# Strassen's algorithm in the last FFN stage of the last two token tiles, for two of four token blocks

## The chip, the cores and the metric

The kernel runs on one core of one Trainium2 chip. The metric is the device time of one execution in microseconds (us). A profiled execution also gives the span from the first to the last instruction, which here is about 2 us shorter than the device time. A difference under 2% counts as "same".

Engines: PE is TensorE's matmuls, PEld its weight loads, DVE is VectorE, ACT is ScalarE, POOL is GpSimd, SP is SyncE, which issues DMA transfers.

## The reference

A sparse attention over 8 x 8 heads, then a multiplicative feed-forward network (FFN) on 4608 tokens:

```python
x = np.ascontiguousarray(attn_out.transpose(0, 2, 1, 3)).reshape(B * S, H * D)   # 4608 x 512
a = x @ w1                   # 512 x 1024
b = x @ w2
h = a * b @ w3               # 1024 x 1024
out = h @ w_out              # 1024 x 512, float32
```

## The kernel before

The kernel folds w3 and w_out into one matrix, `w34` (1024 x 512), so the FFN has two stages: `abt = (x @ w1) * (x @ w2)`, then `out = abt @ w34`. Tokens go in 9 tiles of 512. The last two tiles, tA and tB, already form the first stage by Strassen's algorithm in the form that takes 7 products of half-size blocks for 8 (the Winograd form), for seven of the eight blocks of the hidden dimension (d_ff); one block stays plain. Their last stage is plain, 8 matmuls of 512 columns for each block of 128 tokens (in the last one, split in three column parts):

```python
for ci in range(4 * hf, 4 * hf + 4):
    pin(nc.tensor.matmul(ps, big[("abt", t)][:, ci, bass.ds(ts * P, P)],
                         w34[:, ci, bass.ds(n0, nw)], start=(ci == 0), stop=(ci == KF - 1)))
```

`hf` makes a half-quarter: 4 matmuls, 0.86 us, that can be placed on its own.

Instructions aren't placed by hand. Each is an `op` with an engine, an estimated time, dependencies, buffers and a rank. A planner in the kernel plays these through once and fixes the program order of every engine:

```python
plan = Plan(dict(f=NF, B=2, stg=NSTG, ...))   # buffers: f = 4 single PSUM banks, B = 2 pairs of banks
...
seq = plan.order(slack=cfg.get("slack", 0), ...)
for o in seq:
    o.fn(o.on)
```

The accumulators lie in PSUM, the memory that this program's matmuls write their sums to. A Strassen block has three: A in a single bank (`f`), and E and G together in one two-bank tile (`B`):

```python
def bk(x, kA=kA, kB=kB):
    return bank(*kA) if x == "A" else bank(*kB)[:, "EG".index(x)]
```

The products are P1 (into A), P5 (into G), P6, P7, P4 (into A in turn), P2 (into E) and P3 (into G). Between them, copies and additions on ACT and VectorE: `e` copies A to E after P1, `u2` copies A after P6, `g` adds that to G, `c22` evicts A after P7, `c11` copies E after P2.

The softmax here doesn't subtract the row's maximum and nothing guards it: scores larger than these inputs give would overflow.

## Time and profile before

| | |
|---|---|
| device time, median of 3 runs | 270.85 us (270.61 to 271.14) |
| span of the profiled run | 268.3 us |
| TensorE busy | 256.9 us, 96% |
| first stage of tA and tB | starts at 224.71 us |
| last run of plain last-stage matmuls | 253.00 to 264.43 us, 68 matmuls |
| idle of TensorE in the first stage of tA, tB | about 1.1 us, at 229 to 238 us |

The **tail** is the time from the start of the first plain first-stage matmul of tA (`ps_a`) to the end of the last matmul. Before, it is 264.43 - 224.71 = 39.72 us.

### The profile page before, as it was taken

What the parts mean: (1) busy time and instruction counts of PE and PEld (TensorE: products, weight loads), DVE (VectorE), ACT (ScalarE), POOL (GpSimd) and SP (SyncE); (2) the same over time, 40 slices, a digit from 0 to 9 for tenths busy, and PEclk for the clock granted to TensorE, in tenths of its full rate; (3) what the DMA queues carried; (4) which work ended last, traced back from release to release, by engine and by line L of the source; (5) the groups of instructions that cost most, each with busy time, mean ns of one, the idle gap of its engine ahead of it and who ended that gap; (6) DMA issues with size and microseconds to landing.
All of it is one profiled execution on the core that took longest, in us unless ns stands there. A gap on an engine that the chain in (4) does not pass through costs nothing.

```text
span 268.3 us, 6079 instructions
## 1 busy us (share of the span) xinstructions
PE 256.9 (96%) x2251; PEld 140.3 (52%) x2251; DVE 179.0 (67%) x342; ACT 162.2 (60%) x293; POOL 168.9 (63%) x186
## 2 busy tenths in 40 slices
PE   7878799999999999999999999999999999999994
PEld 2457687545655555554554454455445554434443
DVE  6744565885787748866875788569748865678601
ACT  2780467774766785577477557764775576577241
POOL 6676897779979716955796369716989753900000
PEclk9999999999999999999999999999999999999999
DMA  6999899999799988899999998999996004000053
GB/s 247 322 365 288 294 353 353 326 266 290 255 287 211 175 205 243 188 167 283 228 184 180 264 248 182 189 252 235 162 189 198 2 0 156 0 2 0 0 197 121
DMA packets 72766, 54.41 MB, mean 203 GB/s; under 512 B 44256, under 2 KB 62048, under 8 KB 72736
## 3 DMA queue, kind: packets, MB, share of 16 engines
q1 hardware_dynamic: 72736, 54.02, 83.1%
q8 instruction: 18, 0.29, 0.5%
q14 instruction: 12, 0.10, 0.1%
HBM read 38.93 MB, written 9.44 MB: 180 GB/s over the span
## 4 chain that ended last, share of the span: by engine, by line
PE 86%; DMA 7%; POOL 2%; issue 1%; DVE 1%; ACT 1%; SPq 1%; POOLq 0%; DVEq 0%
PE ps_o L1155 23%; PE ps_b L1135 19%; PE ps_a L1119 18%; DMA st<-in_moe_w_dram 5%; PE ps_Aw L1053 4%; PE ps_S L795 4%; PE ps_Bw L1053 3%; PE ps_mm L670 3%; PE ps_X L843 3%; PE ps_X L831 3%; DMA st<-in_k_dram 2%; PE ps_U L924 2%; PE ps_T L748 2%; POOL w3n L314 1%; SPq L317 1%
## 5 line engine op out<-in xcount | busy, mean ns | idle before, releaser
L1155 PE MATMUL ps_o<-w,abt 128*128 128x512 f16 (+2 forms) x304 | 67.9, 368 | 0.0
L1135 PE MATMUL ps_b<-xT,w2h 128*128 128x512 f16 x232 | 59.4, 379 | 0.2 <-DVE kTL L312 0.2
L1119 PE MATMUL ps_a<-xT,w1h 128*128 128x512 f16 x232 | 59.6, 379 | 0.0
L310 ACT COPY asb<-ps_a 128x512 f32<-128x512 f32 x58 | 33.9, 587 | 30.1 <-PE ps_a L1119 29.0
L1141 DVE TENSOR_TENSOR abt<-ps_b,asb 128x512 f16<-128x512 f32 x58 | 39.9, 688 | 7.8 <-PE ps_b L1135 6.4
L314 POOL CAST xs<-st 80x1024 f16<-80x1024 f32 (+1 forms) x36 | 33.3, 940 | 18.3 <-DMA st<-in_k_dram 10.5
L812 ACT ACTIVATE ps_S<-ps_S 128x576 f32<-128x576 f32 (+2 forms) x56 | 32.8, 627 | 16.4 <-PE ps_S L795 16.4
L1155 PEld LDWEIGHTS <-abt 128*128 128x128 f16 x304 | 27.5, 98 | 28.2 <-issue 0.2
L904 DVE TENSOR_TENSOR xT<-ps_X,rcp 64x288 f16<-64x288 f32 x56 | 25.2, 450 | 18.3 <-ACT rcp L888 17.8
L1135 PEld LDWEIGHTS <-w2h 128*128 128x128 f16 x232 | 21.6, 98 | 23.7 <-issue 0.7
L310 ACT COPY osb<-ps_o 128x512 f32<-128x512 f32 (+1 forms) x36 | 20.2, 580 | 18.7 <-PE ps_o L1155 17.7
L314 POOL CAST v16L<-st 32x768 f16<-32x768 f32 (+1 forms) x32 | 26.3, 821 | 7.3 <-DMA st<-in_v_dram 5.7
L1119 PEld LDWEIGHTS <-w1h 128*128 128x128 f16 x232 | 20.2, 99 | 18.5
L819 DVE TENSOR_TENSOR ptm<-ps_S,maskL 128x576 f16<-128x576 f32 x28 | 19.9, 753 | 9.1 <-ACT ps_S L812 9.0
L867 DVE TENSOR_TENSOR xqs<-ps_X,rcq 96x384 f16<-96x384 f32 (+1 forms) x36 | 20.5, 568 | 1.2
L314 POOL CAST v16S<-st 72x1024 f16<-72x1024 f32 (+1 forms) x16 | 16.5, 1035 | 6.8 <-DMA st<-in_v_dram 6.8
L877 ACT ACTIVATE ps_X<-ps_X 64x576 f32<-64x576 f32 x28 | 17.6, 630 | 3.8 <-PE ps_X L831 3.2
L888 ACT ACTIVATE rcp<-ps_X 64x576 f32<-64x576 f32 x28 | 18.1, 647 | 0.9
L843 PEld LDWEIGHTS <-ptm 128*96 128x96 f16 (+1 forms) x224 | 14.6, 123 | 5.8 <-issue 0.2
L670 PE MATMUL ps_mm<-woh,xT 128*128 128x256 f16 x128 | 16.0, 273 | 1.3 <-POOL woh L314 1.3
L314 POOL CAST x<-st 128x1024 f16<-128x1024 f32 x14 | 14.4, 1036 | 4.4 <-DMA st<-in_k_dram 2.6
L819 DVE TENSOR_TENSOR ptm<-ps_S,maskK 72x576 f16<-72x576 f32 x20 | 14.1, 746 | 2.6 <-ACT ps_S L812 2.6
(113 smaller groups left out, 359.1 us busy)
## 6 DMA issues: line engine op xcount, KB each, us to landing
out_dram<-osb SPq DMA_DIRECT2D x35, 256.0 KB
st<-in_moe_w_dram SPq DMA_DIRECT2D x16, 512.0 KB
st<-in_v_dram SPq DMA_DIRECT2D x16, 288.0 KB
st<-in_v_dram SPq DMA_DIRECT2D x16, 256.0 KB
st<-in_q_dram SPq DMA_DIRECT2D x7, 512.0 KB
st<-in_k_dram SPq DMA_DIRECT2D x7, 512.0 KB
st<-in_q_dram SPq DMA_DIRECT2D x10, 256.0 KB
st<-in_k_dram SPq DMA_DIRECT2D x10, 256.0 KB
```

The lines of the kernel that those rows point to most:

```text
L310: pin(nc.scalar.copy(out=out, in_=in_))
L314: pin(nc.gpsimd.tensor_copy(out=out, in_=in_))
L670: pin(nc.tensor.matmul(ps, w3T(kc)[:, js], big["woh"][:, kc, ns], start=(kc == 0), stop=(kc == KF - 1)))
L812: pin(nc.scalar.activation(out=sps, in_=sps, func=AF.Exp, bias=0.0, scale=scale))
L819: pin(nc.vector.tensor_mul(ptm[0:kr, 0:576].rearrange("p (h a x) -> p h a x", h=2, x=w), pte[0:kr].rearrange("p h (a x) -> p h a x", x=w), ...
L843: pin(nc.tensor.matmul(xps[0:w, h, i * 65:(i + 1) * 65], ptms[pslot][0:kr, c0:c0 + w], vt[0:kr, 2 * (hp % 2) + h, g * m + i, 0:D + 1], sta ...
L867: pin(nc.vector.tensor_mul(xqs[0:w, 0:m].rearrange("p i h d -> p h i d"), xv[:, :, :, 0:D], _ap(rcp, 0, [[rcp.ap[0][0], w], [4, 2], [1, m] ...
L904: pin(nc.vector.tensor_mul(o, i0, i1))
L1119: pin(nc.tensor.matmul(ps, w1h[:, ci, js], xT[ci][:, tok], start=(ci == 0), stop=(ci == KM - 1)))
L1135: pin(nc.tensor.matmul(ps, w2h[:, ci, js], xT[ci][:, tok], start=(ci == 0), stop=(ci == KM - 1)))
L1141: pin(nc.vector.tensor_mul(big[("abt", t)][:, jc, :], bank("f", f"b{t}_{jc}"), live[("asb", t, jc)]))
L1155: pin(nc.tensor.matmul(ps, big[("abt", t)][:, ci, bass.ds(ts * P, P)], w34[:, ci, bass.ds(n0, nw)], start=(ci == 0), stop=(ci == KF - 1)))
```

## The change

Token blocks 0 and 1 of both tiles leave the plain last stage and go as two Strassen blocks: 7 products of 4 matmuls of 256 columns instead of 16 matmuls of 512. The left factors are sums of parts of abt (Z1, Z2, Z4 on VectorE, Z3 on POOL), the right factors differences of parts of w34 (on POOL). The plain d_ff block of the first stage moves from 0 to 7, so that the first half of the hidden dimension is finished earlier.

```diff
-  sf=(1, 2, 3, 4, 5, 6, 7), ...
+  sf=(0, 1, 2, 3, 4, 5, 6), ..., so=(0, 1), ro=42)
...
+    def out_strassen():
+        HN = DM // 2
+        hh = {(1, 1): (tA, 0), (1, 2): (tA, 4), (2, 1): (tB, 0), (2, 2): (tB, 4)}
+        W = {(i, j): w34[:, 4 * i - 4:4 * i, bass.ds(HN * (j - 1), HN)] for i in (1, 2) for j in (1, 2)}
...
+            def bk(x, kA=kA, kB=kB):
+                return (bank(*kA) if x == "A" else bank(*kB)[:, "EG".index(x)])[:, 0:HN]
...
+                    for c in range(4):
+                        pin(nc.tensor.matmul(bk(x), lf()[:, c], rt()[:, c], start=st_ and c == 0, stop=c == 3,
+                                             skip_group_check=not st_))
+
+                return plan.op(f"{nm}o{ts}", {"PE": 440}, fn, deps=d + list(extra), take=take,
+                               rank=100 + 24 * tA + cfg.get('ro', 30) + 3 * n_ + rank, soft=True)
...
+            q1 = prod("P1", take=[kA], extra=sfirst)
+            q5 = prod("P5", take=[kB], extra=[q1], rank=.1)
+            ce_ = vec("e", AC, lambda e, bk=bk: copy(e, bk("E"), bk("A")), [q1, q5])
+            q6 = prod("P6", extra=[ce_], rank=.5)
+            q2 = prod("P2", extra=[ce_], rank=.6)
+            cu = vec("u2", AC, ... copy(e, new("u2"), bk("A")), [q6], take=["u2"])
+            q7 = prod("P7", extra=[cu], rank=1)
+            g = vec("u4", DV, ... tensor_add(bk("G"), bk("G"), tmp["u2"]), [cu, c5], give=[tk["u2"]])
+            c22 = vec("c22", DV, ... tensor_add(new("o8")[:, HN:DM], bk("A"), tmp["p5"]), [q7, c5], ...)
+            c11 = vec("c11", AD, ... copy(e, new("o7")[:, 0:HN], bk("E")), [q2], take=["o7"])
+            q3 = prod("P3", extra=[g], rank=1.1)
+            q4 = prod("P4", extra=[c22], rank=1.2)
...
         for ts in range(NT // P):
+            if t in zs and ts in SO:
+                continue
```

(A renamed dictionary key in the attention part has no effect on the program.)

More of the change, by code (lines that the diff above doesn't have):

```diff
@@ L41 @@
            pord=lambda b: (2, 3, 0, 1) if b < 2 else (0, 1, 2, 3), tsplit=False, dmaf=1.08, nhr=8, cast=dict(w1=dict(POOL=1040)),
-           first=('DVE', 'ACT', 'POOL'), early=0, pm=4, nx=4, nstg=8, new=(2, 3), lb=3, ll=4, nat={'POOL': 1160}, sf=(1, 2, 3, 4, 5, 6, 7), te={'POOL': 2150}, nr=(1, 25, 2, 0), te1='POOL', se=((3, 0), (3, 1), (1, 0), (2, 0), (4, 0)))
+           first=('DVE', 'ACT', 'POOL'), early=0, pm=4, nx=4, nstg=8, new=(2, 3), lb=3, ll=4, nat={'POOL': 1160}, sf=(0, 1, 2, 3, 4, 5, 6), te={'POOL': 2150}, nr=(1, 25, 2, 0), te1='POOL', se=((3, 0), (3, 1), (1, 0), (2, 0), (4, 0)), so=(0, 1), ro=42)
 def _ap(t: bass.AP, off_add, dims):
@@ L302 @@
     plan = Plan(dict(f=NF, B=2, stg=NSTG, asb=2, osb=3, rcp=2, xqs=2, xqd=cfg.get("nxq", 2), w3n=3, abt=NABT,
-                     u2=2, p5=2, c11=2, c22=2))
+                     u2=2, p5=2, c11=2, c22=2, ob=4))
     def pin(ins):
@@ L580, in fn @@
                 copy(e, t.rearrange("p c h d -> p h c d"), stg[key][0:nr])
-                x16[(b, nm, hp)] = t
+                x16[(b, nm, "s", hp)] = t
             c = cast("c" + key, key, ds, {"POOL": 825} if local else POOL, fn)
@@ L594, in ft @@
                 pin(nc.sync.dma_start(o.rearrange("x (c w) -> x c w", w=nr),
-                                      x16[(b, nm, hp)].rearrange("p c h d -> p (c h d)"), transpose=True))
+                                      x16[(b, nm, "s", hp)].rearrange("p c h d -> p (c h d)"), transpose=True))
             o = DTop[(b, nm, hp)] = plan.op(f"D{nm}{b}_{hp}", {"SP": 1300}, ft, deps=[c], dma=cfg.get("dtc", (1080, 1200))[0 if local else 1], store=True,
@@ L947 @@
     tk1, tk2 = bass.ds(tA * NT, NT), bass.ds(tB * NT, NT)
-    smul, sfirst = {}, []
+    smul, sfirst, mul = {}, [], {}
     if SF:
@@ L1003 @@
                 T[(i, 1)].deps.append(gate)
+        T1last = T[(4, 1)]
         SL = lambda j: (lambda c: St[j // 3][:, (j - 1) % 2 if j < 3 else j - 3, c])
@@ L1092, with ftt, ah, sv @@
         smul[(tA, jc)], smul[(tB, jc)] = h1, h2
+    SO = cfg.get("so", ()) if SF else ()
+    def out_strassen():
+        HN = DM // 2
+        hh = {(1, 1): (tA, 0), (1, 2): (tA, 4), (2, 1): (tB, 0), (2, 2): (tB, 4)}
+        W = {(i, j): w34[:, 4 * i - 4:4 * i, bass.ds(HN * (j - 1), HN)] for i in (1, 2) for j in (1, 2)}
+        T, Tt = {}, {}
+        for i, x, y in ((1, (1, 2), (1, 1)), (3, (2, 2), (1, 2)), (2, (2, 2), 1), (4, (2, 1), 2)):
+            def ftt(e, i=i, x=x, y=y):
+                if i in (1, 2):
+                    raw = stgs[plan.slot[("stg", f"O{i}")]].bitcast(FP16).rearrange("p (i k n) -> p i k n", i=2, k=4)
+                    Tt[i], Tt[{1: 3, 2: 4}[i]] = raw[:, 0], raw[:, 1]
+                b0 = Tt[y] if isinstance(y, int) else W[y]
+                eng = nc.gpsimd if e == "POOL" else nc.vector
+                pin(eng.tensor_sub(Tt[i], W[x], b0))
+            T[i] = plan.op(f"O{i}", {"POOL": 2150}, ftt, deps=w34op + [T1last, T.get(1), T.get(2)],
+                           take=[("stg", f"O{i}")] if i in (1, 2) else [], rank=14, lock=True)
+        def ah(i, j, ts):
+            t, c0 = hh[(i, j)]
+            return big[("abt", t)][:, c0:c0 + 4, bass.ds(ts * P, P)]
+        def sv(i, ts):
+            return xT[i - 1][:, 0:4 * NT].rearrange("p (k n) -> p k n", k=4)[:, :, bass.ds(ts * P, P)]
+        md = lambda t, k: [mul[(t, jc)] for jc in range(4 * k - 4, 4 * k)]
+        for n_, ts in enumerate(SO):
+            Sx = {}
+            for i in (3, 1, 2, 4):
+                def fss(e, i=i, ts=ts):
+                    eng = nc.gpsimd if e == "POOL" else nc.vector
+                    f = eng.tensor_add if i == 1 else eng.tensor_sub
+                    a0 = {3: lambda: ah(1, 1, ts), 1: lambda: ah(2, 1, ts), 2: lambda: sv(1, ts), 4: lambda: ah(1, 2, ts)}
+                    a1 = {3: lambda: ah(2, 1, ts), 1: lambda: ah(2, 2, ts), 2: lambda: ah(1, 1, ts), 4: lambda: sv(2, ts)}
+                    pin(f(sv(i, ts), a0[i](), a1[i]()))
+                d = {3: md(tA, 1) + md(tB, 1), 1: md(tB, 1) + md(tB, 2), 2: md(tA, 1), 4: md(tA, 2)}[i]
+                Sx[i] = plan.op(f"Z{i}_{ts}", {"POOL": 1150} if i == 3 else {"DVE": 430}, fss,
+                                deps=d + ([Sx[i // 2]] if i in (2, 4) else []), rank=3.9 + .01 * n_, lock=True)
+            kA, kB = ("f", f"Ao{ts}"), ("B", f"Bo{ts}")
+            prods = dict(P1=(lambda ts=ts: ah(1, 1, ts), lambda: W[(1, 1)], "A", md(tA, 1) + w34op),
+                         P5=(lambda ts=ts: sv(1, ts), lambda: Tt[1], "G", [Sx[1], T[1]]),
+                         P6=(lambda ts=ts: sv(2, ts), lambda: Tt[2], "A", [Sx[2], T[2]]),
+                         P2=(lambda ts=ts: ah(1, 2, ts), lambda: W[(2, 1)], "E", md(tA, 2)),
+                         P7=(lambda ts=ts: sv(3, ts), lambda: Tt[3], "A", [Sx[3], T[3]]),
+                         P4=(lambda ts=ts: ah(2, 2, ts), lambda: Tt[4], "A", md(tB, 2) + [T[4]]),
+                         P3=(lambda ts=ts: sv(4, ts), lambda: W[(2, 2)], "G", [Sx[4]]))
+            tmp = {}
+            def bk(x, kA=kA, kB=kB):
+                return (bank(*kA) if x == "A" else bank(*kB)[:, "EG".index(x)])[:, 0:HN]
+            def new(nm, tmp=tmp, ts=ts):
+                if nm[0] == "o":
+                    tmp[nm] = xT[plan.slot[("ob", f"{nm}o{ts}")]][:, 4 * NT:6 * NT].bitcast(FP32)
+                else:
+                    tmp[nm] = qkp.tile([P, HN], FP32, tag=TAG[nm], bufs=2, name=nm)
+                return tmp[nm]
+            def prod(nm, extra=(), take=(), rank=0, ts=ts, kA=kA, kB=kB, prods=prods, bk=bk):
+                lf, rt, x, d = prods[nm]
+                def fn(e):
+                    if nm == "P1":
+                        bank(*kA, [P, NT], FP32)
+                    if nm == "P5":
+                        live[kB] = seen[plan.slot[kB]]
+                    st_ = nm in ("P1", "P5")
+                    for c in range(4):
[3 more added lines that the diff above has]
+                               rank=100 + 24 * tA + cfg.get('ro', 30) + 3 * n_ + rank, soft=True)
+            def vec(nm, eng, fn, deps, give=(), take=()):
+                return plan.op(f"{nm}o{ts}", eng, fn, deps=deps, give=list(give),
+                               take=[("ob" if x[0] == "o" else x, f"{x}o{ts}") for x in take], rank=3 + .1 * n_)
+            AC, DV, AD = {"ACT": 370}, {"DVE": 400}, {"ACT": 370, "DVE": 380}
+            tk = {x: ("ob" if x[0] == "o" else x, f"{x}o{ts}") for x in ("u2", "p5", "o7", "o8")}
+            q1 = prod("P1", take=[kA], extra=sfirst)
+            q5 = prod("P5", take=[kB], extra=[q1], rank=.1)
+            ce_ = vec("e", AC, lambda e, bk=bk: copy(e, bk("E"), bk("A")), [q1, q5])
+            q6 = prod("P6", extra=[ce_], rank=.5)
+            c5 = vec("p5", AC, lambda e, bk=bk, new=new: copy(e, new("p5"), bk("G")), [q5], take=["p5"])
+            q2 = prod("P2", extra=[ce_], rank=.6)
+            cu = vec("u2", AC, lambda e, bk=bk, new=new: copy(e, new("u2"), bk("A")), [q6], take=["u2"])
+            q7 = prod("P7", extra=[cu], rank=1)
+            g = vec("u4", DV, lambda e, bk=bk, tmp=tmp: pin(nc.vector.tensor_add(bk("G"), bk("G"), tmp["u2"])),
+                    [cu, c5], give=[tk["u2"]])
+            c22 = vec("c22", DV, lambda e, bk=bk, new=new, tmp=tmp: pin(
+                nc.vector.tensor_add(new("o8")[:, HN:DM], bk("A"), tmp["p5"])), [q7, c5], take=["o8"], give=[tk["p5"]])
+            c11 = vec("c11", AD, lambda e, bk=bk, new=new: copy(e, new("o7")[:, 0:HN], bk("E")), [q2], take=["o7"])
+            q3 = prod("P3", extra=[g], rank=1.1)
+            q4 = prod("P4", extra=[c22], rank=1.2)
+            c12 = vec("c12", AD, lambda e, bk=bk, tmp=tmp: copy(e, tmp["o7"][:, HN:DM], bk("G")), [q3, c11], give=[kB])
+            c21 = vec("c21", AD, lambda e, bk=bk, tmp=tmp: copy(e, tmp["o8"][:, 0:HN], bk("A")), [q4, c22], give=[kA])
+            for t, o, c in ((tA, "o7", c12), (tB, "o8", c21)):
+                plan.op(f"st{o}_{ts}", {"SP": 450}, lambda e, o=o, t=t, ts=ts, tmp=tmp: pin(
+                    nc.sync.dma_start(out_r[t * (NT // P) + ts], tmp[o])), deps=[c], give=[tk[o]], rank=4.5, dma=750,
+                        store=True)
@@ L1144 @@
                                 give=[("f", f"b{t}_{jc}"), ("asb", f"{t}_{jc}")], rank=4))
+        if t in zs:
+            mul.update({(t, jc): m for jc, m in enumerate(muls)})
+        if SO and t == tB:
+            out_strassen()
         for ts in range(NT // P):
+            if t in zs and ts in SO:
+                continue
             last = t == NTILE - 1 and ts == NT // P - 1
```

## The prediction

> **What bounds the kernel now.** I began with the page: the engine totals and the row of slices.
>
> ```profile
> PE 256.9 (96%) x2251; PEld 140.3 (52%) x2251; DVE 179.0 (67%) x342; ACT 162.2 (60%) x293; POOL 168.9 (63%) x186
> ...
> PE   7878799999999999999999999999999999999994
> ...
> DVE  6744565885787748866875788569748865678601
> ...
> POOL 6676897779979716955796369716989753900000
> PEclk9999999999999999999999999999999999999999
> ```
>
> TensorE is busy for 96% of the 268.3 us span and its row is at 9 to the last slice (6.7 us each). POOL is idle in the last five slices, VectorE nearly so in the last two. The clock is full throughout, so a matmul saved is worth its full-speed time and nothing changes by throttling. The change touches only the end, so next I read the chain that ended last, in order of time, over that part.
>
> ```profile
> 233.65 0.88 PE ps_Bw L1053 x4
> 234.53 0.02 issue
> 234.55 0.58 ACT ps_Bw L310
> ...
> 236.42 0.59 ACT c L310
> 237.01 0.02 issue
> 237.04 0.71 DVE ps_Bw L1076
> ...
> 250.09 0.86 PE ps_o L1155 x4
> 250.95 0.43 PE ps_Aw L1053 x2
> 251.38 0.43 PE ps_Bw L1053 x2
> 251.82 0.92 PE ps_o L1155 x4
> 252.74 0.43 PE ps_Aw L1053 x2
> 253.17 10.83 PE ps_o L1155 x60
> ```
>
> ps_Aw and ps_Bw are the existing Strassen products of the first FFN stage, ps_o is the last stage. After one hiccup at 234.5 to 237.8 us, where ACT and VectorE stand in the chain, it is TensorE back to back to 264 us: every ps_o matmul is on the path. Two of the three pieces of ps_o that stand between Strassen products are shown: the scheduler uses the last stage as filler. From the timeline of TensorE, the last plain run starts at 253.00 us and holds 68 matmuls in 11.43 us. After it come a copy of the last output columns, the last store, and the end of the span at 268.3.
>
> **What the skill says, and whether the trace agrees.** The Trainium skill, "TensorE: Matmul & The Clock Gate", section "Wait — 56ns, not 53.3ns?", gives the start-to-start time of warm matmuls as N ÷ 2.4 GHz plus about 2.5 ns. The trace agrees for N = 512: 0.86 us for 4, 216 ns each. Whether it holds at N = 256, where each matmul still needs a new 128-column weight, decides this case. The timeline of TensorE has such a stream earlier in this kernel:
>
> ```profile
> 32.43 1.91 PE L670 MATMUL ps_mm<-woh,xT 128*128 128x256 f16 x16
> ...
> 37.12 1.58 PE L670 MATMUL ps_mm<-woh,xT 128*128 128x256 f16 x13
> ...
> 43.46 1.05 PE L670 MATMUL ps_mm<-woh,xT 128*128 128x256 f16 x8
> ```
>
> One such matmul is recorded as 272 ns (drain included), so the spacing is (1910 - 272)/15 = 109 ns, and (1580 - 272)/12 = 109 ns. The formula gives 256/2.4 + 2.5 = 109.2. Weight loads (98 ns recorded) are hidden. "SBUF — State Buffer", section "SBUF: two separate sides", says that a VectorE instruction with two SBUF inputs and a GpSimd one that reads SBUF lock each other out. The new fp16 sums on VectorE are of that kind, the PSUM evictions are not. The trace agrees for the evictions: they take 0.68 to 0.70 us both while POOL forms weight differences (225.8 to 234.3 us) and after it.
>
> **The change, part by part.** The d_ff block left plain moves from 0 to 7. There are still seven Strassen blocks and one plain block per tile with the same ranks in the queue, so this costs TensorE nothing. It lets the first four d_ff blocks of both tiles be complete after four Strassen blocks, which the new sums need.
>
> Removed on TensorE: token blocks 0 and 1 of both tiles, 4 x 8 = 32 matmuls of N = 512: 32 x 216 = 6.91 us. Added: 2 x 7 products of 4 matmuls, N = 256: 56 x 109 = 6.10 us. Difference: -0.81 us, all of it on the path if TensorE stays fed.
>
> Added on POOL: four weight differences of 1024 elements per partition (2.13 us each, from the group of the existing ones) and two sums at 1.15 us: 4 x 2.13 + 2 x 1.15 = 10.8 us. POOL is free from 234.3 us, so the weights are ready near 243 and all is done near 246, while the first product that uses them starts after 254. Hidden.
>
> Added on VectorE, per token block: three fp16 sums at 0.42 (the group of the existing ones) and two fp32 additions of 256 columns. Those I estimate at 0.69 - 256 x 1.04 ns = 0.42 us, the slope from its copies of 128 and 256 columns (292 and 425 ns). Together 2.1 us. ACT: copies of 256 columns, which I estimate at 265 + 128 x (580 - 265)/384 = 370 ns from its 128- and 512-column copies. Three are fixed on ACT and three go to ACT or VectorE, so 2.2 us against the two copies of 0.58 us that go. One token block has 28 x 109 = 3.05 us of TensorE, so neither engine binds by volume.
>
> The latency inside one block is the danger. Its longest path is P1, P5, copy, P6, copy, P7, addition, P4: five products of 0.44 us, evictions of 0.37 + 0.37 + 0.42, and three handovers of about 0.26 us (about 0.16 of drain plus 0.1 of signalling, read from the starts around 234.5 us). That is 2.20 + 1.16 + 0.78 = 4.14 us against 3.05 us of own work: 1.1 us of holes per block, 2.2 us for both, if nothing fills them.
>
> Fill: each block can fill the other, and so can the plain quarters of both tiles. By the ranks, tile A's quarters 2 and 3 come first, then Strassen 0 and 1, then tile B's quarters 2 and 3 (3.46 us). When the last first-stage product ends (253.0 us), I expect two half-quarters of tile A to be left, 1.73 us. The sum for P5 needs the last product of the first stage evicted (VectorE free at 253.9) and 0.42 us of its own, so P5 can start at 254.4, before the fill is out at 254.7. Carrying the handovers on by hand, with half-quarters of tile B where both blocks wait, I find no hole over 0.1 us. The last P4 comes about 261.7, followed by 1.7 us of tile B's quarter 3, so the end is as before: three narrow parts, copy, store.
>
> Sum: -0.81 on TensorE, plus 0.15 us for holes that my hand schedule misses (the existing Strassen stage has about 1.1 us of them in 28 us, nearly all in its start-up): -0.66 us. 270.85 - 0.66 = 270.2.
>
> **Rivals.** (1) Handovers win: both blocks wait at once and the program order, fixed beforehand, has no ready work at that point. For it: the hiccup at 234.5 us, where just such a chain of copies and an addition stopped TensorE. Against it: from 238 to 253 us the same pattern runs without a hole. Fully unfilled it is -0.81 + 2.2 = +1.4, 272.2 us; half of it gives 271.1. (2) VectorE becomes the bound. It is busy 6.21 of the 7 us from 240 to 247 (89%), but only 1.1 of 11.5 from 253 on, where the new work falls. If its queue holds the first sums 0.5 us longer, the gain shrinks to 0.2: 270.6. (3) The end moves: a Strassen output instead of a narrow part comes last, with a wider copy and store. I give it 0.3 to 0.5 us, hence 270.5 to 270.7. (4) The start-up hiccup, whose order is set anew, changes by itself: up to 0.5 us either way. A DMA bound is not a rival: engines move 0.40 of capacity after 253 us, and stores stay the same in bytes.
>
> **Range and chances.** The gain can't exceed 0.81 us except through rival 4 and the spread of the three runs (270.61 to 271.14). So the low end is 269.6. Rivals 2 and 3 together, or half of rival 1, give 270.9 to 271.1; I take 270.9. A change of 2% is 5.4 us, over twice the worst sum here, so the verdict is almost surely "same".
>
> **What would show it right or wrong.** Right: TensorE has 24 more matmuls; the 256-column ones space at 109 ns; from about 253 us no idle before a product over 0.2 us; the last matmul about 0.7 us earlier; POOL busy to about 246 us and never the releaser of a product. Wrong: holes before P6, P7 or P4 ended by ACT or VectorE, a first P5 that waits for its sum, spacing nearer 120 ns (then 56 x 11 ns = 0.6 us of the gain is gone), or a last matmul that is not a narrow part of tile B.

## More of the kernel before

The slices of the page and the chain that ended last are shown in the prediction. They say that TensorE has work without a break nearly to the end, so the length of the end is the number of its matmuls times their spacing plus any hole.

## The result

In the four runs of the first comparison the changed kernel took 270.17 us (269.85 to 270.72) against 270.73 us (270.36 to 271.14). The ratio is 0.9981 with a 95% interval of 0.9959 to 1.0004. A ratio is the mean time of one kernel's fast runs over that of the other's of the same rounds, so it isn't quite the ratio of the medians. The predicted 270.2 was met to 0.03 us. The interval includes 1, though, and the profile doesn't show the gain where the prediction put it.

The page of the changed kernel, engine totals and slices:

```profile
PE 255.9 (95%) x2275; PEld 142.3 (53%) x2275; DVE 184.5 (69%) x356; ACT 162.6 (61%) x297; POOL 179.8 (67%) x192
...
PE   6778799999999999999999999999999999999984
...
DVE  6745566885786758866875787479748865677842
...
POOL 6676896779989726965796279527999453994000
```

The 24 additional matmuls are there (2275 for 2251). POOL now works through two of the slices that were empty before, VectorE works more in the last three. In the part that the change touches, the only mark against it is one digit: TensorE's slice before the last has fallen from 9 to 8. (The first and the second digit are lower by one as well, long before that part.)

The timeline of TensorE (start, duration, line, what it writes and reads, count; the bracket is idle time and what ended it) shows what is behind that digit:

```profile
251.53 0.60 PE L1167 MATMUL ps_Ao<-w,abt 128*128 128x256 f16 x4
252.13 0.59 PE L1054 MATMUL ps_Aw<-xT,st 128*128 128x512 f16 x2
...
256.89 0.60 PE L1167 MATMUL ps_Bw<-st,xT 128*128 128x256 f16 x4
257.33 0.60 PE L1167 MATMUL ps_Ao<-st,xT 128*128 128x256 f16 x4
258.05 0.60 PE L1167 MATMUL ps_Bw<-w,xT 128*128 128x256 f16 x4
...
259.80 0.60 PE L1167 MATMUL ps_Ao<-st,xT 128*128 128x256 f16 x4
261.01 0.60 PE L1167 MATMUL ps_Bw<-w,xT 128*128 128x256 f16 x4 [0.61 <-DVE xT L312]
...
262.75 1.93 PE L1268 MATMUL ps_o<-w,abt 128*128 128x256 f16 x24
```

Products that follow each other closely start 0.44 us apart (256.89 to 257.33), that is 109 ns for each matmul, as predicted. But three starts are further apart than that. From 251.53 to 252.13 there are 0.60 us, a hole of 0.16. From 257.33 to 258.05 there are 0.72, a hole of 0.28. From 259.80 to 261.01 there are 1.21, a hole of 0.77. (The bracket gives 0.61 because the recorded duration includes 0.16 us of drain.) The sum is 1.21 us. The first stage starts at 224.53 us, and the last matmul ends at 262.75 + 1.93 = 264.68. So the tail is 40.15 us. The prediction's terms with the holes give 39.72 - 0.81 + 1.21 = 40.12. **In the profile the change has made the tail 0.43 us longer.**

What stands in the holes is in the chain that ended last (start, duration, what):

```profile
257.17 0.44 DVE ps_Bw L1187
257.61 0.02 issue
257.63 0.38 ACT xT L310
258.01 0.04 issue
258.05 0.60 PE ps_Bw L1167 x4
...
260.07 0.44 DVE ps_Bw L1187
260.51 0.02 issue
260.54 0.43 DVE xT L312
260.97 0.04 issue
261.01 0.60 PE ps_Bw L1167 x4
```

L1187 is the addition `g` into G. P3, which accumulates on G, needs it. But P3 doesn't start when `g` is done, at 257.6 and 260.5. It starts after one more copy, `xT<-ps_Bw`, which is `c11`, the copy of **E**. P3 has nothing to do with E, and the planner doesn't list it among P3's dependencies. At build time the framework can list reasons for its waits. That listing can't be checked here; it named these: `g` waits for P2, `c11` for `g` and P3 for `c11`, each as an overlap on the tile that holds E and G. The chain above shows the same order in time, and the run e_sep below tests it.

### The profile page after: what moved, and what is told of

Same layout as the page of the kernel before. It is cut to its first block, busy times and chain, and to the rows that moved or that the text cites. A ratio compares the mean times of both kernels' runs of the same rounds, so it can differ in the third digit from the quotient of the medians.

```text
span 268.4 us, 6153 instructions
## 1 busy us (share of the span) xinstructions
PE 255.9 (95%) x2275; PEld 142.3 (53%) x2275; DVE 184.5 (69%) x356; ACT 162.6 (61%) x297; POOL 179.8 (67%) x192
## 3 DMA queue, kind: packets, MB, share of 16 engines
HBM read 38.93 MB, written 9.44 MB: 180 GB/s over the span
## 4 chain that ended last, share of the span: by engine, by line
PE 85%; DMA 7%; SPq 2%; DVE 1%; POOL 1%; ACT 1%; issue 1%; POOLq 0%; DVEq 0%
PE ps_o L1268 20%; PE ps_b L1242 19%; PE ps_a L1226 18%; DMA st<-in_moe_w_dram 7%; PE ps_Aw L1054 4%; PE ps_S L795 4%; PE ps_Bw L1054 3%; PE ps_mm L670 3%; PE ps_X L843 3%; PE ps_X L831 3%; PE ps_U L924 2%; SPq L317 2%; PE ps_T L748 2%; POOL w3n L314 1%; PE ps_Ao L1167 1%; PE ps_Bw L1167 1%
## 5 line engine op out<-in xcount | busy, mean ns | idle before, releaser
L1268 PE MATMUL ps_o<-w,abt 128*128 128x512 f16 (+2 forms) x272 | 61.3, 367 | 0.0
L1268 PEld LDWEIGHTS <-abt 128*128 128x128 f16 x272 | 24.4, 98 | 23.7
L310 ACT COPY osb<-ps_o 128x512 f32<-128x512 f32 (+1 forms) x32 | 17.9, 580 | 15.7 <-PE ps_o L1268 15.6
```

The costliest lines, as they stand in the source:

```text
L310: pin(nc.scalar.copy(out=out, in_=in_))
```

## The experiments

Theory A: the matmul saving is real, and holes eat it. A1: the two holes before P3 come from waits between E and G, which share a tile and no data. Rivals: (B) the holes are the plain latency of handing results from engine to engine; (C) there is a real gain of 0.5 us and the profile fell badly; and moving the plain block does something by itself. Every run gave a correct result. The kernel before was timed in the same rounds.

**a_again.** No edit.

> The changed kernel once more, unedited, to learn its true distance from the kernel before. I measure the tail from the first matmul of the last plain first-stage block to the end of the last matmul: 39.72 us before, 40.15 us after in the two profiles. Theory A (the 0.81 us saved on TensorE is eaten by new holes of 0.16 + 0.28 + 0.77 = 1.21 us): tail again about 40.15, and the timed difference is not really a gain: between 0 and +0.5 us, ratio 1.000 to 1.002. Theory C (the measured 0.5 us is the matmul saving, the profile fell badly): ratio 0.998 again, tail near 39.2 in this profile.

Tail 264.72 - 224.57 = 40.15 us. The time was 270.34 us against 270.22, ratio 1.0001 (0.998 to 1.0022). The holes belong to the program and not to one execution, and the 0.5 us gain didn't come back. Theory C falls by the tail, for which it had 39.2; the interval of the ratio alone still reaches 0.998.

**m_moveonly.** Only the plain block moved:

```diff
-so=(0, 1), ro=42
+so=(), ro=42
```

> Only the first part of the change: d_ff block 7 plain instead of block 0, no Strassen in the last stage. Theory A: no effect, tail 39.7 and ratio 1.000 within 0.001, so the whole cost and gain lies in the Strassen products of the last stage. Rival: the moved block itself changes the start-up of the first stage (1.1 us of idle there before), by up to 0.5 us either way, ratio 0.998 or 1.002.

Tail 264.38 - 224.66 = 39.72 us, exactly as before; ratio 1.0013 (0.9993 to 1.0032). Moving the plain block leaves the tail as it was. All gain and cost in the tail lie in the Strassen products.

**e_sep.** E in a bank of its own:

```diff
+            kE = ("f", f"Eo{ts}")
             def bk(x, kA=kA, kB=kB):
-                return (bank(*kA) if x == "A" else bank(*kB)[:, "EG".index(x)])[:, 0:HN]
+                return (bank(*kA) if x == "A" else bank(*kE) if x == "E" else bank(*kB)[:, 1])[:, 0:HN]
...
-            ce_ = vec("e", AC, ... copy(e, bk("E"), bk("A")), [q1, q5])
+            ce_ = plan.op(f"eo{ts}", AC, fe_, deps=[q1, q5], take=[kE], ...)    # fe_ allocates E, then copies
-            c11 = ... [q2], take=["o7"])
+            c11 = ... [q2], take=["o7"], give=[kE])
```

> Same program order on every engine, same operations; only the accumulator E (P1+P2) of each Strassen block of the last stage gets a single-bank PSUM tile of its own, where it shared a two-bank tile with accumulator G. Theory A1 (the holes before P3 come from waits that the shared tile makes between E and G, which share no data): the holes of 0.28 and 0.77 us go, the tail is 40.15 - 1.05 = 39.1 us, ratio to before about 0.998, 1.0 us better than the unedited changed kernel. Theory B (the holes are the plain handover latency of copies and additions between products): nothing changes, tail 40.15, same time as the unedited changed kernel.

In the traces the order is the same on all five engines, instruction for instruction, apart from the tile's name (and the semaphore instructions). So this run takes the waits away and, besides, only puts E in another bank; late_p1 below gets rid of the holes without that. Its chain at the place of the two holes:

```profile
257.83 0.44 PE ps_Bw L1173 x4
258.27 0.44 PE ps_Ao L1173 x4
258.70 0.44 PE ps_Bw L1173 x4
259.14 0.87 PE ps_Ao L1173 x8
260.01 0.44 PE ps_Eo L1173 x4
260.45 0.44 PE ps_Ao L1173 x4
260.89 0.44 PE ps_Bw L1173 x4
261.32 0.86 PE ps_o L1274 x4
```

No other engine stands between the products. P3 (258.70 and 260.89) follows directly on P7. Tail 264.39 - 225.30 = 39.09 us for 39.1 expected; ratio 0.9971 (0.9951 to 0.9992). Against the unedited changed kernel on the same chip, in the same rounds, the mean time is 0.77 us lower. The handovers that were really needed (`u2` to `g` to P3) are all still there and cost nothing. B falls, A1 stands. The waits weren't needed for PSUM either: the Trainium skill, "PSUM — Partial Sum Buffer", section "PSUM bank collisions raise a hardware error", says to guard PSUM by bank and quadrant, by bank as the simple version. E and G lie in different banks in both kernels. The run agrees: with those waits gone the result is correct.

**q_told.** The same tile and the same waits, but the planner is told of them, and P1 no longer serves as filler:

```diff
-            q1 = prod("P1", take=[kA], extra=sfirst)
+            q1 = prod("P1", take=[kA], extra=sfirst + [Sx[1]])      # Sx[1] is the sum Z1
-            g   = ... [cu, c5]
+            g   = ... [cu, c5, q2]
-            c11 = ... [q2]
+            c11 = ... [q2, g]
-            q3 = prod("P3", extra=[g], rank=1.1)
+            q3 = prod("P3", extra=[c11], rank=1.1)
```

> Same buffers as the changed kernel, so the same waits between E and G, but the planner is told of them (addition into G after P2, copy of E after that addition, P3 after that copy) and P1 waits for the first VectorE sum, so that it isn't used as a filler that is too short. Theory A (holes, whatever their cause, cost only because nothing was planned into them): all three holes go, tail 40.15 - 1.2 = 38.95 us, ratio about 0.997. Theory B2 (TensorE is bound by the chain of one block even when other work is put in between, or the end moves to a wide copy and store): tail above 39.5, ratio 0.999 or more.

Tail 263.55 - 224.62 = 38.93 us for 38.95 expected: all three holes gone. But the ratio is only 0.9991 (0.996 to 1.0022; one of six runs took 272.17 us). The gain was lost after the last matmul. The timeline of the DMA issues shows it (start, duration of the run of issues, queue, count):

```profile
260.91 3.11 SPq L1198 DMA_DIRECT2D out_dram<-xT  x4
264.11 1.38 SPq L1289 DMA_DIRECT2D out_dram<-osb  x3
```

L1198 are the four Strassen output stores, L1289 the three narrow last ones. The new order finishes both Strassen blocks late and close together, so SP is still issuing their stores when the narrow parts are ready (the first copy is done at 263.57). The fourth Strassen issue alone took 1.12 us, where most of SP's output stores took 0.33 to 0.50; why isn't known. The last issue ends at 265.49, 1.94 us after the last matmul. In the kernel before it is 1.40.

**q_act.** The run q_told with the Strassen stores issued from ACT's queue:

```diff
-plan.op(f"st{o}_{ts}", {"SP": 450}, ... nc.sync.dma_start(
+plan.op(f"st{o}_{ts}", {"ACT": 100}, ... nc.scalar.dma_start(
```

> The run q_told with one edit: the four Strassen output stores are issued from the ACT queue, the plain ones stay on SP. In q_told the last matmul came 0.79 us earlier than in the kernel before (38.93 against 39.72 us), but the last store was issued 1.94 us after it instead of 1.40, because SP was still issuing four Strassen stores one by one. Theory D (the order of issue on SP gives 0.5 us back): last store issued about 1.4 us after the last matmul, ratio to before near 0.997. Rival (the store traffic itself is the limit at the end): last issue earlier but the span after the last matmul stays at 4.6 us, ratio 0.999 again.

```profile
260.67 2.29 ACTq L1198 DMA_DIRECT2D out_dram<-xT  x4
263.35 1.44 SPq L1289 DMA_DIRECT2D out_dram<-osb  x3
```

Tail 38.93 us again. The last issue now ends 264.79 - 263.31 = 1.48 us after the last matmul, and the span ends 4.34 us after the last matmul instead of 4.69 (3.89 in the kernel before). So 0.46 us of issue came back, and 0.35 of it shows at the end of the span. The 0.1 between them is no finding: from the last issue to the end of the span two profiles of one kernel (e_sep, e_sep_2) differ by 0.3. Theory D is right on the issue; its rival, that the end stays at 4.6 us, isn't borne out, though the end of the kernel before isn't reached. The ratio is 0.9949 (0.9924 to 0.9975), on another chip than q_told. The Trainium skill, "DMA: Bandwidth & Descriptors", section "Issuing engines are not separate DMA queues", says that issuing from several engines saves only the sequencer's time to issue, as all run on the same 16 DMA engines. That agrees: the time from the last issue to the end of the span did not shrink (2.85 against 2.75 us).

**late_p1.** Only the P1 edit of q_told; buffers, waits and the planner's ignorance are those of the changed kernel:

```diff
-            q1 = prod("P1", take=[kA], extra=sfirst)
+            q1 = prod("P1", take=[kA], extra=sfirst + [Sx[1]])
```

> One edit to the changed kernel: P1 of both blocks waits for the first VectorE sum, so that it is no longer a filler inside the first stage. Buffers and the planner's knowledge are as in the changed kernel; but the two blocks now start together and interleave, so each wait between E and G falls while the other block has products ready. Theory A (a hole appears only where the next product in the fixed order is the waiting one): no hole over 0.1 us, tail 40.15 - 1.2 = 38.95 us, ratio to before 0.997 if the end follows. Rival: the waits bind whatever stands between, tail 39.9 us, only the 0.2 us around the early P1 gained.

Tail 263.20 - 224.28 = 38.92 us, no hole over 0.1 us. The last issue ends 1.40 us after the last matmul; ratio 0.9942 (0.9913 to 0.997). From its timeline:

```profile
256.91 0.60 PE L1167 MATMUL ps_Ao<-st,xT 128*128 128x256 f16 x4
257.35 0.60 PE L1167 MATMUL ps_Bw<-w,abt 128*128 128x256 f16 x4
257.78 0.60 PE L1167 MATMUL ps_Ao<-st,xT 128*128 128x256 f16 x4
258.22 0.60 PE L1167 MATMUL ps_Bw<-w,abt 128*128 128x256 f16 x4
258.65 0.60 PE L1167 MATMUL ps_Ao<-st,xT 128*128 128x256 f16 x4
259.09 0.60 PE L1167 MATMUL ps_Bw<-w,xT 128*128 128x256 f16 x4
```

With both P1 at the same point, the two blocks run side by side: P6 and P2 of one block, then of the other, then P7 and P3 (the six lines above, 0.43 or 0.44 us apart). Each wait of one block passes while the other's products run. The waits are all still in the program and cost nothing.

**swap_late.** The P1 edit, and P2 placed before P6:

```diff
-            q2 = prod("P2", extra=[ce_], rank=.6)
+            q2 = prod("P2", extra=[ce_], rank=.4)
```

> The late_p1 edit and P2 ahead of P6 in each block, so that both waits of the E and G pair fall on work that is done anyway. Theory A: no hole, tail 38.95 us; the last P4 comes about 1.9 us before the last matmul, so SP is free for the narrow stores and the last store is issued 1.4 us after the last matmul; ratio 0.997. Rival: with P6 later, the path P6, copy, P7, addition, P4 is longer by 0.44 us per block and TensorE idles before P7 or P4, tail above 39.3.

Tail 264.31 - 225.39 = 38.92 us, so its rival (a longer path through P6) falls. The last part of the expectation was wrong: the last issue ends 1.80 us after the last matmul, not 1.4, with SP issuing Strassen stores until 264.68 (here too the fourth issue was long, 0.99 us). Ratio 0.9956 (0.9928 to 0.9985). No better than late_p1.

**one_block.**

```diff
-so=(0, 1)
+so=(0,)
```

> Strassen in the last stage for token block 0 only, otherwise as the changed kernel. Half the matmul saving: 16 x 216 - 28 x 109 = 0.40 us. By the planned order a plain half-quarter stands before each waiting product and the copy of E comes ahead of the addition into G, so theory A gives no new hole: tail 39.72 - 0.40 = 39.32 us, better than the changed kernel with two blocks (40.15). Rival (holes belong to the Strassen chain and come with every block, 0.6 us each): tail 39.9 us.

Tail 264.74 - 225.41 = 39.33 us for 39.32 expected; ratio 0.9974 (0.9948 to 1.0001). One block with plain work among its products saves its 0.40 us in full. In the profile it was better than two blocks with the waits in the wrong place.

**a_third, e_sep_2, late_2** repeat three of these on one chip.

> The changed kernel unedited, beside e_sep_2 and late_2 on one chip, because the start of the tail moved between 224.3 and 225.4 us from run to run and the kernel before scattered from 269.75 to 273.08 us in the last job. From the tail (40.15 against 39.72 us) and the end: between 0 and +0.4 us of the kernel before, ratio 1.000 to 1.0015.

> The changed kernel with E in a bank of its own, again. Tail 39.1 us; 0.6 us below the kernel before and 1.0 us below the changed kernel: ratio 0.9977 to before, 0.996 to the changed kernel.

> The changed kernel with only P1 made late, again. Tail 38.92 us, last store issued 1.4 us after the last matmul: 0.8 us below the kernel before, 1.2 us below the changed kernel: ratio 0.997 to before. The 0.9942 of the last job is 0.7 us more than the tail explains; if that was the scatter of the kernel before, it comes back to 0.997 here.

The tails came as expected: 40.14, 39.09 and 38.92 us. The ratios came lower than expected, 0.999, 0.9953 and 0.9957; the last two intervals just include the expected 0.9977 and 0.997. The last issue of late_2 was expected 1.4 us after the last matmul and came at 1.66, so that figure doesn't repeat as the tail does.

**null_before** is the kernel before against itself.

> The kernel before, unedited, timed against itself. In three jobs the changed kernels came out about 0.5 us better against the kernel before than their tails say. If the way of comparing favours the kernel under test, this ratio is about 0.998 too; if not, it is 1.000 within 0.002 and the 0.5 us lies in the kernels or their scatter. Its tail should be 39.72 us again; its start of the tail shows whether 224.7 us is typical of it.

All runs together; "to the end" is the span's end less the start of the tail, and it includes the last stores:

| kernel | tail, us | last issue after last matmul | to the end | ratio to before |
|---|---|---|---|---|
| before | 39.72 | 1.40 | 43.6 | |
| null_before | 39.72 | 1.51 | 43.6 | 1.0007 (0.9974 to 1.0039) |
| m_moveonly | 39.72 | 1.39 | 43.5 | 1.0013 (0.9993 to 1.0032) |
| changed | 40.15 | 1.34 | 43.9 | 0.9981 (0.9959 to 1.0004) |
| a_again | 40.15 | 1.35 | 43.9 | 1.0001 (0.998 to 1.0022) |
| a_third | 40.14 | 1.35 | 43.9 | 0.999 (0.9965 to 1.0015) |
| one_block | 39.33 | 1.36 | 43.1 | 0.9974 (0.9948 to 1.0001) |
| e_sep | 39.09 | 1.34 | 43.3 | 0.9971 (0.9951 to 0.9992) |
| e_sep_2 | 39.09 | 1.36 | 43.0 | 0.9953 (0.9927 to 0.9979) |
| q_told | 38.93 | 1.94 | 43.6 | 0.9991 (0.996 to 1.0022) |
| q_act | 38.93 | 1.48 | 43.3 | 0.9949 (0.9924 to 0.9975) |
| swap_late | 38.92 | 1.80 | 43.5 | 0.9956 (0.9928 to 0.9985) |
| late_p1 | 38.92 | 1.40 | 42.8 | 0.9942 (0.9913 to 0.997) |
| late_2 | 38.92 | 1.66 | 43.0 | 0.9957 (0.9934 to 0.998) |

The tail repeats to 0.01 us, while the timed runs don't repeat to 0.5. In the profiles what varies is mostly the part before the tail. Its length was 224.71 and 223.96 us in two profiles of the same kernel before, and 223.96 to 225.54 over all runs; the spans of the kernel before ranged from 267.4 to 269.7 us in the null test. That test shows no bias of the comparison, but its interval of 0.0065 is wider than the effect of the change.

late_p1 beats both kernels. Its two intervals against the kernel before exclude 1 (so do those of both e_sep runs), and in the last job its median was 269.69 us against 270.44 for the changed kernel and 271.10 for the kernel before. It is one edited line.

The clean comparison is with the changed kernel on the same chip. By the mean times e_sep was 0.77 us below it, e_sep_2 0.91 and late_2 0.90 (each within 0.5 to 0.7 us, at 95%, from six runs a side). Tail and end together say 0.63, 0.91 and 0.91. There the traces explain the times.

What stays open is the distance to the kernel before. Every comparison of a kernel with Strassen products in the last stage came out lower against it than tail and end explain, by 0.2 to 1.1 us (most in swap_late and q_act), and m_moveonly and the null test came out 0.5 and 0.2 higher. So the changed kernel is level with the kernel before or better, where its tail says 0.4 us worse. With the scatter of the part before the tail this may be chance, though the sign is the same in all eleven comparisons (those of one job share their runs of the kernel before). In the profiles the part before the tail isn't shorter with the Strassen products, and I didn't find a cause.

## Why the prediction was right or wrong

The predicted time was right, and the sum that led to it was not.

- **What bounds the kernel** was right. TensorE's order of work sets the end, and each hole in it shows up in full.
- **Moving the plain block costs nothing**: right, 39.72 us with that part alone.
- **32 x 216 ns out, 56 x 109 ns in, -0.81 us**: right. Without holes the tail is 38.92 us, 0.80 us shorter. One block gave 0.39 us.
- **POOL**: right. The weight differences are done at 242.6 us (predicted 243), the sums at 245.7 (246), and POOL stands in no hole. VectorE's new sums began only at 253.48, so no run shows whether the two engines lock each other out there.
- **VectorE and ACT by volume**: right. The additions of 256 columns took 0.41 to 0.43 us (0.42), the copies 0.37 to 0.38 (0.37). Rival 2 didn't occur: the first sums didn't hold up P5.
- **The start of P5**: two half-quarters of tile A were left, and P5 started at 254.28 us with no hole before it (predicted 254.4 at the earliest, 254.7 in the plan). Right.
- **"I find no hole over 0.1 us"** is the step that failed. Three holes came, 0.16 + 0.28 + 0.77 = 1.21 us, where the sum had 0.15. My hand schedule followed the dependencies that the planner lists. It missed that the framework makes E and G wait for each other because they share a tile. So it had `g` waiting only for `u2`, and P3 only for `g`. In truth P3 of the second block waited for P2, `g` and `c11` in a row, while a half-quarter that could have run stood behind it in the fixed order. P3 isn't on the longest path that I wrote down, nor among the products whose holes would have shown me wrong (P6, P7, P4). The chain of the kernel before already showed such a wait, in the hiccup at 236.4 us that I quoted: an ACT copy `c` (of E) and then, at 237.04, VectorE's addition into `ps_Bw` (G). What that addition reads, `u`, had been ready since 236.38 (its line is at the end of this section). I read it as start-up latency. The smallest hole came from an order that I didn't work out: with P1 (0.44 us) instead of a half-quarter (0.86 us) as filler, TensorE waited for the eviction after P7 of the last first-stage block.
- **Rival 1** named the right mechanism in general (the fixed order has no ready work at that point) and the right size: "half of it gives 271.1". In the profile that is what happened, at +0.43 us. I gave it too little weight.
- **Rival 3** (the end moves) didn't occur in the changed kernel: narrow parts came last and the last issue kept its distance (1.34 us). It came in another form in q_told, once the holes were closed, as 0.5 us of store issue.
- **Why the time was met all the same**: predicted -0.66 us, measured -0.56 by the medians, but two later comparisons gave ratios of 1.0001 and 0.999. The early part of the kernel varies by more than the change is worth. The hit was luck: the scatter is broader than what was predicted. What the runs support is that the changed kernel can't be told from the one before, and that its saving is lost in holes.

The two copies of ACT that come before that addition in the kernel before, from the timeline of ACT:

```profile
235.80 0.58 ACT L310 COPY u<-ps_Aw 128x512 f32<-128x512 f32 x1
236.42 0.58 ACT L310 COPY c<-ps_Bw 128x512 f32<-128x512 f32 x1
```

## What to carry to other kernels

When a fixed program order is planned from a list of dependencies, that list must contain the waits that the framework will really make. Accumulators that share a tile can wait for each other without sharing data; give each its own tile, or tell the planner, or place two independent chains side by side so that the waits pass in each other's shadow. When a change is worth less than the scatter of the run, measure the stretch that it touches in the trace, from a fixed instruction to a fixed instruction: here that repeated to 0.01 us. And look past the last matmul: work that is finished earlier but in a bunch can queue for the issue of its stores.

## What the Trainium skill lacked or had wrong

- "TensorE: Matmul & The Clock Gate", section "Back-to-back issue gap": it puts the sustained spacing in a stream of weight load and matmul pairs at about 131 ns for 512 columns and 81 ns for 128, and calls N/2.4 + 2.5 an isolated gap. The runs show the formula in such streams: 216 ns for 512 columns (0.86 us for 4), 109 ns for 256 (0.44 us for 4), and 56 ns for 128. The last comes from the final 24 matmuls: 1.93 us less the last one's recorded 0.22 is 1.71; less 8 x 0.109, over 15 spacings.
- None has it: waits that software makes between two accumulators in different banks of one PSUM tile. They made holes of 0.28 and 0.77 us here, which went when one accumulator got a tile of its own. "PSUM — Partial Sum Buffer" says that guarding by bank suffices.
- "DMA: Bandwidth & Descriptors", section "Issuing engines are not separate DMA queues", calls the issue time usually small next to the transfer, which no run here contradicts, but gives no figure for it. Here one store's issue took 0.33 to 1.12 us, and stores queue for it: in q_told the last issue ended 1.94 us after the last matmul, for 1.40 in the kernel before, and a second issuing engine brought 0.46 us of it back.
